# One tile for both accumulators of a spectral product, and scan rotations with a signed sine table (gated S5 + H3 mix, one core)

## The chip, the core and the metric

One core of one Trainium2 chip. The kernel is launched once; its time is the device time of that launch in microseconds (us), taken as the median of several runs. The kernel before takes 382.55 us (three runs, 381.49 to 382.69). A profile of one further execution gives each instruction's start and duration on the engines: PE (TensorE matmul), PEld (its weight loads), DVE (VectorE), ACT (ScalarE), POOL (GpSimd, which here mostly issues adding DMAs) and SP (the queue from which nearly all loads and stores are issued).

## What is computed

Two sequence mixers over 2048 steps and 1024 channels are blended by a gate. With `x` of shape [2048, 1024]:

```python
g   = sigmoid((x * gate_w).sum(-1))
# a: diagonal complex state space (S5), 1024 states
Bu  = x @ B_bar.T ;  h[t] = Lam_bar * h[t-1] + Bu[t] ;  a = 2 Re(h @ C.T) + x * Dskip
# b: H3: short convolution of k, times v, then a long convolution by FFT, times x
kv  = (4-tap conv of B_k) * B_v ;  b = x * (fftconv(kv, B_ssm_k) + kv * B_ssm_D)
out = g * a + (1 - g) * b
```

## The kernel before

**Order of work.** A helper `put` (line 92) chains every compute and queue instruction to the previous one of the same engine, so each engine runs its instructions in the order in which the Python code issues them; nothing is reordered later. Because all of them go through this helper, the profile names line 94 for nearly every row, and one tells groups apart by tile names. `move` and `load_t` (a DMA that transposes) go to SP's queue, `gather` is a DMA from POOL that adds its source into its destination.

**First half: H3, channel block by channel block (c = 0 to 7).** Per block of 128 channels the short convolution (`taps`), the spectra of kernel and signal (`fwd_K` into tile `Kh`, `fwd_V` into `Vh`), their complex block product, and the inverse transform (`inverse`, tile `psz`) are made. Both spectra have a real and an imaginary part (index `c`), four overlap blocks (`b`) and 512 columns. `products` (line 680) forms the product on DVE: accumulator `G` for the real part of K times V, accumulator `T2` (in the room of `BT[3]`) for the imaginary part. Each takes multiplies of 4096, 3072, 2048 and 1024 elements per partition and adds; one add, `G += n1`, is done by a `gather` DMA. Then `T2` is combined with `G`, and sum and difference of its halves are written to `G`, which `inverse` reads. It is a Python generator: each `yield` is a point at which the main loop (line 1136) puts other work of that block in between, `times_v` among it. `times_v` multiplies the convolved k by v (tile `ks`), mirrors it on PE (`lo`), makes `ev` on DVE and `ks += lo` by a `gather`; `fwd_V` on PE needs both. Kernel spectra of even blocks lie in `BT[2]`, of odd ones in the pool `kvh`. Interleaved with this are the first `Bu` products of the state space mixer and `turn_table` (line 461), in which ACT makes cosine and sine tables.

**Second half: S5.** Time is cut into four blocks (tb) of 512 steps, states into four groups (g) of 256. `Bu(i)` takes 32 matmuls of 512 columns per `i` (tile `both`, from `xT[tb]` and `BT[g]`); the list `order` (line 788) maps `i` to (tb, g). `turn_U` then adds the odd steps' neighbours to the even ones with ACT (`Q`) and two `gather`s (`U<-Q`). `scan` (line 913) rotates U by the cosine and sine tables, runs four recurrences (`tensor_tensor_scan`), rotates back into `hb` and updates the odd steps. `Cy` (tile `psy`) multiplies states by C. The lists `plan` and `turned` (lines 1390 to 1393) say which `Bu`, `turn_U` and `Cy` stand between scan j and scan j + 1.

**SP's queue around the change.** `xT` of time blocks 0 and 3 share one buffer (`xt_first`, line 78), so `load_xT(3)` waits for the last `Bu` with tb = 0. Before, `Bu(7)` is (0, 3), and `load_xT(3)` stands at line 1334, after `Bu(7)` and ahead of the last `inverse`, the loads of C (CT4 to CT7, lines 1353 to 1358) and the row loads `loads(0)` to `loads(2)`. `load_BT(3, ...)` stands at lines 1300 and 1301, ahead of the loads of C for states 1 to 3. `Bu(12)` is (3, 0), the first user of `xT[3]`; `plan` puts it at j = 3.

Of the kernel before, what the change touches and what calls it, by code (L numbers as in the profile page):

```python
# [20 lines left out]
def kernel(  # L21
# [115 lines left out]
    kv_pool = h3pool(h3, "kvh", 3)  # L137
    g_pool = h3pool(h3, "gh", 2)
    cv_pool = h3pool(h3, "cv", 2)
    tab_pool = h3pool(h3, "tab", 1)  # L140
    WK = h3pool(h3, "wkh", 1).tile([128, 2, 3072], BF16, name="wkh")
# [5 lines left out]
    zeros = WK[:, 0, 0:512]  # L147
# [254 lines left out]
    TCS = rot_pool.tile([128, NP, 2, HB], BF16, name="TCS")  # L402
    TC, TS = TCS[:, :, 0], TCS[:, :, 1]
# [72 lines left out]
    KH, VH, GH = {}, {}, {}  # L476
# [136 lines left out]
    def spectrum(which, c):  # L613
        if which == "K" and c % 2 == 0:

            t = BT[2].rearrange("p c d q -> p (c d q)")
        elif which == "G":
            t = whole[c] = g_pool.tile([128, 4096], BF16, name="G")
        else:
            t = kv_pool.tile([128, 4096], BF16, name=which + "h", tag="kvh")  # L620
# [59 lines left out]
    def products(c, h=0, home=u4, by_dma=True):  # L680

        if c not in GH:
            GH[c] = spectrum("G", c)
        K, Vt, G = (x[c][h].rearrange("p c b f d -> p c b (f d)") for x in (KH, VH, GH))
        w = K.shape[3]
        T2s = kv_pool.tile([128, 4096], BF16, name="t2", tag="kvh") if c == NC - 1 else BT[3].rearrange("p c d q -> p (c d q)")
        T2 = T2s[:, h * 2048:h * 2048 + 8 * w]
        W1, W2 = (WK[:, i, h * 1536:h * 1536 + 6 * w] for i in range(2))

        def mult(a, k, room, t=None):  # L690

            full = [128, 2, 4 - a, w]
            if t is None:
                t = room.rearrange("p (c b x) -> p c b x", c=2, x=w)
            tt(t, bc(K[:, k:k + 1, a:a + 1], full), Vt[:, :, 0:4 - a], ALU.mult)
            return t

        if c == 0 and h == 0:

            for f in range(2):  # L700
                k_, v_, g_ = (x[c][h][:, :, :, f] for x in (KH, VH, GH))
                tt(g_, bc(k_[:, 0:1, 0:1], [128, 2, 4, 128]), v_, ALU.mult)
        else:
            mult(0, 0, None, G)
        yield
        n1 = mult(1, 0, W1)
        if by_dma:
            gather(G[:, :, 1:], n1)
        yield
        t2 = mult(0, 1, T2)  # L710
        yield
        n2 = mult(1, 1, W2)
        if not by_dma:
            tt(G[:, :, 1:], G[:, :, 1:], n1, ALU.add)
        if c == NC - 1:
            yield
        n3 = mult(2, 1, home([128, 4 * w], BF16, "t"))
        tt(t2[:, :, 1:], t2[:, :, 1:], n2, ALU.add)
        n2 = mult(3, 1, home([128, 2 * w], BF16, "t"))
        tt(t2[:, :, 2:], t2[:, :, 2:], n3, ALU.add)  # L720
        n1 = mult(2, 0, W2[:, 0:4 * w])
        n3 = mult(3, 0, W2[:, 4 * w:])
        tt(t2[:, :, 3:], t2[:, :, 3:], n2, ALU.add)
        tt(n1[:, :, 1:], n1[:, :, 1:], n3, ALU.add)
        yield
        tt(G[:, :, 2:], G[:, :, 2:], n1, ALU.add)
        yield
        tt(t2[:, 1], G[:, 0], t2[:, 1], ALU.subtract)
        tt(t2[:, 0], G[:, 1], t2[:, 0], ALU.add)
        if c == 0 and h == 0:  # L730
            return
        lo, hi = ((t2[:, :, :, 0:256], t2[:, :, :, 256:512]) if c > 0 else
                  [T2s[:, i * 2048:(i + 1) * 2048].rearrange("p (c b x) -> p c b x", c=2, x=256) for i in range(2)])
        to = whole[c].rearrange("p (a c b x) -> p a c b x", a=2, c=2, b=4)
        tt(to[:, 0], lo, hi, ALU.subtract)
        tt(to[:, 1], lo, hi, ALU.add)

    def inverse(c):

        del GH[c]  # L740
        G = whole.pop(c).rearrange("p (a c b f d) -> p a c b f d", a=2, c=2, b=4, d=128)
        for par in range(2):
            ps = ps2([128, 2, 4, 128], "psz")
            for j in range(2):
                tl = 2 * par + j
                for fi in range(2):
                    for cc, tab in enumerate((CI, SI)):
                        mm(ps[:, j], tab[:, fi, tl * 128:(tl + 1) * 128], G[:, par, 1 - cc, :, fi],
                           fi == 0 and cc == 0, fi == 1 and cc == 1)
            cv = cv_pool.tile([128, 2, 4, 128], BF16, name="cv")  # L750
            act(cv, ps, func=ACT.Copy)
            move(cv_scr[c, :, 2 * par:2 * par + 2], cv)
            yield
# [34 lines left out]
    order = [(0, 0), (0, 1), (1, 0), (1, 1), (2, 0), (2, 1), (0, 2), (0, 3), (1, 2), (1, 3), (2, 2), (2, 3)]  # L788
# [16 lines left out]
    def Bu(i):  # L805
# [7 lines left out]
        if i in (10, 11):  # L813
            if i == 10:
                s5p["u2"] = xt_pool.tile([128, 2, 2 * (4 * HB + 4)], BF16, name="U2", tag="xT")
            U = s5p["u2"][:, i - 10]
# [96 lines left out]
    def scan(tb, g, fin):  # L913
# [4 lines left out]
        A = w2([128, 2, 2, HB], BF16, "A")  # L918
        W = None

        for js in ([slice(0, 1), slice(1, 2)] if last else [slice(0, 2)]):
# [6 lines left out]
            b = w2([128, 2, 2, HB], BF16, "trn")[:, :, js]  # L928
            tt(b, bc(TS[:, g2][:, None], full), Uj, ALU.mult)
# [4 lines left out]
            tt(Aj[:, 0], Aj[:, 0], b[:, 1], ALU.add)  # L934
            tt(Aj[:, 1], Aj[:, 1], b[:, 0], ALU.subtract)
            if W is None:
                W = w2([128, 2, 2, HB], BF16, "W")
            for j in range(js.start, js.stop):
                pi = 2 * g + j
                for c in range(2):  # L940
                    put("dve", V.tensor_tensor_scan, out=W[:, c, j], data0=bc(rv2[:, pi:pi + 1], [128, HB]),
                        data1=A[:, c, j], initial=0.0 if tb == 0 else init[tb][:, c, pi:pi + 1],
                        op0=ALU.mult, op1=ALU.add)
# [6 lines left out]
            Wj = W[:, :, js]  # L950
            tt(hb, bc(TC[:, g2][:, None], full), Wj, ALU.mult)
            if tb < NTB - 1:
                copy(WL[tb][:, :, g2], Wj[:, :, :, HB - 1])
            b = w2([128, 2, 2, HB], BF16, "trn")[:, :, js]
            tt(b, bc(TS[:, g2][:, None], full), Wj, ALU.mult)
            if not last:
                yield
            tt(hb[:, 0], hb[:, 0], b[:, 1], ALU.subtract)
            tt(hb[:, 1], hb[:, 1], b[:, 0], ALU.add)
# [4 lines left out]
            if by_act and tb == NTB - 1:  # L964
                q = [s5p["Q"].tile([128, 2, 2, HB], BF16, name="Q") for k in range(2)]
            else:
                q = [w2([128, 2, 2, HB], BF16, "q") for k in range(2)]
# [168 lines left out]
    for c in range(NC - 1):  # L1136
# [43 lines left out]
        steps(prod, 3)  # L1180
# [119 lines left out]
    load_BT(3, 0)  # L1300
    load_BT(3, 1)
# [4 lines left out]
    with tc.tile_pool(name="fin", bufs=1, side="right") as fin:  # L1306
# [16 lines left out]
        steps(prod, 2)  # L1323
        b6, b7 = Bu(6)
# [9 lines left out]
        load_xT(3)  # L1334
# [7 lines left out]
    wk = pool("wk", 5)  # L1342
# [5 lines left out]

    def w2(shape, dt, name):
        return wk.tile(shape, dt, name=name, tag="w2")  # L1350
# [39 lines left out]
    plan = ["", "B9 B10", "B11", "B12 B13 C0", "C1", "C2", "C3 B14", "B15", "G10", "G11", "G12 G13", "G20", "G21 G22 G23",  # L1390
            "", "", ""]
    turned = dict(zip(range(3, 12), (8, 9, 4, 10, 11, 12, 13, 14, 15)))
    turned[0] = 7
# [46 lines left out]
    for j in range(NS):  # L1440
# [109 lines left out]
```

## Time and profile before

| | value |
|---|---|
| median of 3 runs | 382.55 us |
| span of the profiled execution (first to last instruction) | 380.0 us |
| matmuls recorded on PE | 2435 |
| instructions on DVE | 595 |
| bytes moved by DMA | 71.78 MB |

A profile row of a group gives line, engine, operation, tiles (out<-in), shape (partitions x elements), count, then busy time in us, mean duration in ns, and the idle time before it with what ended it. A row of the timeline gives start, duration and count. Durations of neighbours on DVE overlap a little: an instruction starts some 80 ns before the one ahead of it is through, so steps are read from start to start. A matmul of 512 columns is listed with 379 ns, but the next one starts after 0.216 us.

### The profile page before, as it was taken

How to read it: one execution, taken by the hardware profiler on the slowest of the kernel's cores; microseconds unless marked ns; L12 is line 12 of the kernel's file. 1: busy time of each engine (PE TensorE's matmuls, PEld its weight loads, DVE VectorE, ACT ScalarE, POOL GpSimd, SP SyncE). 2: the span in 40 equal slices, each digit the busy share in tenths (PEclk: the TensorE clock that was granted, in tenths of full speed). 3: DMA queues.
4: the chain of work that ended last, by engine and by line, in shares of the span. 5: the costliest groups of instructions: out<-in, count | busy, mean ns of one | idle time of the engine just before them, and what ended most of it. 6: DMA issues, size and time to landing. Idle time of an engine off the chain costs nothing.

```text
span 380.0 us, 6673 instructions
## 1 busy us (share of the span) xinstructions
PE 371.0 (98%) x2435; PEld 201.2 (53%) x2469; DVE 369.6 (97%) x595; ACT 309.0 (81%) x475; POOL 78.9 (21%) x109
## 2 busy tenths in 40 slices
PE   8999999999999999999999999999999999999995
PEld 5656357575584856654454444444444444444444
DVE  8899999999999999999999999999999999999996
ACT  5879997988989999786949999996989769937621
POOL 4011030110301103021002012122415323635000
PEclk9999999999999999999999999999999999999999
DMA  7989999998999998969999999967899999999902
GB/s 168 167 112 248 213 216 227 219 195 206 226 175 192 227 177 170 184 145 151 194 206 190 204 209 253 240 137 135 158 226 181 237 254 220 153 255 155 218 0 110
DMA packets 126259, 71.78 MB, mean 189 GB/s; under 512 B 104649, under 2 KB 107601, under 8 KB 126226
## 3 DMA queue, kind: packets, MB, share of 16 engines
q1 hardware_dynamic: 112416, 45.90, 55.9%
q0 software_dynamic: 12688, 25.17, 38.9%
q10 hardware_dynamic: 1122, 0.28, 0.4%
q8 instruction: 19, 0.31, 0.3%
q14 instruction: 14, 0.11, 0.1%
HBM read 15.48 MB, written 8.39 MB: 63 GB/s over the span
## 4 chain that ended last, share of the span: by engine, by line
PE 44%; DMA 19%; DVE 17%; issue 11%; ACT 6%; POOL 1%; SPq 0%; DVEq 0%; POOLq 0%; ACTq 0%
PE both L94 16%; PE psk L94 7%; DMA U<-Q 5%; PE taps L94 5%; PE psv L94 5%; PE psz L94 4%; DMA kT<-in_B_k_dram 3%; DVE BT L94 3%; PE even L94 3%; DVE W L94 3%; PE odd L94 2%; PE foldk L94 2%; DMA ks<-lo 2%; DMA out_dram<-m 2%; DVE hb L94 2%
## 5 line engine op out<-in xcount | busy, mean ns | idle before, releaser
L94 PEld LDWEIGHTS <-BT 128*128 128x128 bf16 x640 | 62.1, 98 | 48.3 <-issue 0.2
L94 PE MATMUL both<-xT,BT 128*128 128x512 bf16 x375 | 83.0, 379 | 0.4
L94 POOL DMA_DIRECT2D U<-Q x26 | 26.4, 1027 | 82.5 <-ACT Q L94 39.9
L94 PEld LDWEIGHTS <-hb 128*128 128x128 bf16 x256 | 24.9, 98 | 30.2 <-issue 0.5
L94 PEld LDWEIGHTS <-U 128*128 128x128 bf16 x252 | 24.6, 98 | 27.4
L94 PE MATMUL psy<-CT,hb 128*128 128x512 bf16 x157 | 36.5, 379 | 0.1
L94 ACT ACTIVATE Vh<-psv 128x1024 bf16<-128x1024 f32 x32 | 30.7, 1034 | 6.2 <-PE psv L94 6.2
L94 PE MATMUL psy<-CT,U 128*128 128x512 bf16 (+1 forms) x156 | 34.7, 368 | 0.2
L94 ACT ACTIVATE U<-both 128x512 bf16<-128x512 f32 x44 | 24.2, 594 | 10.2 <-PE both L94 9.9
L94 DVE TENSOR_TENSOR_SCAN W<-rv,init,A 128x256 bf16<-128x256 f32 x48 | 32.2, 730 | 0.0
L94 POOL DMA_DIRECT2D G<-wkh x8 | 9.7, 1218 | 101.4 <-DVE wkh L94 101.4
L94 ACT ACTIVATE Q<-U,lam 128x512 bf16<-128x512 bf16 (+1 forms) x52 | 29.9, 612 | 0.0
L94 PE MATMUL psk<-eok,SF 128*128 128x384 bf16 (+1 forms) x119 | 28.2, 354 | 0.3
L94 PEld LDWEIGHTS <-SF 128*128 128x128 bf16 x184 | 18.0, 98 | 19.4 <-issue 0.7
L94 PE MATMUL psz<-G,CI 128*128 128x512 bf16 x64 | 24.3, 379 | 0.1
L94 PE MATMUL psz<-G,SI 128*128 128x512 bf16 x64 | 24.3, 379 | 0.0
L94 PE MATMUL taps<-dg,kT 128*128 128x128 bf16 (+1 forms) x352 | 22.2, 213 | 1.0 <-DMA kT<-kT 0.7
L94 PEld LDWEIGHTS <-kT 128*128 128x128 bf16 x352 | 21.7, 102 | 2.6 <-DMA kT<-in_B_k_dram 1.2
L94 PE MATMUL psy<-CTa,hb 128*128 128x512 bf16 x94 | 22.6, 379 | 0.2
L94 DVE TENSOR_TENSOR wkh<-BT,Vh 128x3072 bf16<-128x3072 bf16 (+4 forms) x20 | 21.8, 1109 | 0.0
L94 DVE TENSOR_TENSOR wkh<-Kh,Vh 128x3072 bf16<-128x3072 bf16 (+2 forms) x16 | 21.3, 1349 | 0.0
L94 PE MATMUL psy<-CTa,U 128*128 128x512 bf16 (+1 forms) x91 | 20.7, 370 | 0.1
(230 smaller groups left out, 838.0 us busy)
## 6 DMA issues: line engine op xcount, KB each, us to landing
U<-Q POOLq DMA_DIRECT2D x26, 256.0 KB, 4.9
G<-wkh POOLq DMA_DIRECT2D x6, 768.0 KB, 8.3
cv_scr<-cv SPq DMA_DIRECT2D x16, 256.0 KB, 6.0
kn<-in_B_ssm_k_dram SPq DMA_DIRECT2D x5, 512.0 KB, 4.5
v<-in_B_v_dram SPq DMA_DIRECT2D x5, 512.0 KB, 4.5
out_dram<-m SPq DMA_DIRECT2D x8, 256.0 KB, 4.3
BT<-cv_scr SPq DMA_DIRECT2D x7, 256.0 KB, 7.3
out_dram<-BT SPq DMA_DIRECT2D x7, 256.0 KB, 2.0
```

What stands on the lines that cost most here:

```text
L94: i = f(*a, **kw)
```

## The change

- `products`: both accumulators lie in one tile `sums` [128, 2, 4096]; each multiply covers real and imaginary part of K at once (8192, 6144, 4096 and 2048 elements). The `gather` still adds 3072 elements of the first accumulator; the second one's same add is done by DVE right behind it. Sum and difference go back into V's own tile, so the `G` pool is gone, and `kvh` has two buffers for V alone.
- Kernel spectra of odd blocks lie in `BT[3]`, so `load_BT(3)` moves behind the multiplies of the last block, after the loads of C 1 to 3.
- `turn_table` makes a second, negated sine table; `scan` uses both with the real and imaginary parts of its input swapped, so that each rotation is two multiplies and one full-width add (1024 elements) in place of two adds of 512. The recurrences write over their input, and the rotation tiles serve as room for the update of the odd steps.
- `order`: `Bu(6)`, `(7)`, `(8)` become (0, 2), (1, 2), (2, 2), and (0, 3), (1, 3), (2, 3) follow as `Bu(9)` to `(11)`. `plan` puts `Bu(9)` at j = 0, and `turned` puts its `turn_U` at j = 1. `load_xT(3)` moves to the end of j = 0.

```diff
-        T2s = kv_pool.tile(...) if c == NC - 1 else BT[3].rearrange("p c d q -> p (c d q)")
+        A = sums[:, :, h * 2048:h * 2048 + 8 * w].rearrange("p k (c b x) -> p k c b x", c=2, x=w)
+        def mult(a, t):
+            ...
+            k_ = bc(K[:, :, a:a + 1], [128, 2, 8 - 2 * a, w])
+            v_ = bc(Vt[:, :, 0:4 - a].rearrange("p c b x -> p c (b x)")[:, None], [128, 2, 2, (4 - a) * w])
+            tt(t, k_, v_, ALU.mult)
+            return t
...
+            mult(0, sums[:, :, h * 2048:h * 2048 + 8 * w])
+        yield
+        n1 = mult(1, WK[:, h * 3072:h * 3072 + 12 * w])
         if by_dma:
-            gather(G[:, :, 1:], n1)
+            gather(A[:, 0, :, 1:], n1[:, 0])
         yield
...
+        if by_dma:
+            tt(A[:, 1, :, 1:], A[:, 1, :, 1:], n1[:, 1], ALU.add)
+        else:
+            tt(A[:, :, :, 1:], A[:, :, :, 1:], n1, ALU.add)
+        yield
+        n2 = mult(2, WK[:, 3072:7168] if c > 0 else home([128, 8 * w], BF16, "t"))
+        n3 = mult(3, home([128, 4 * w], BF16, "t"))
+        yield
+        tt(n2[:, :, :, 1:], n2[:, :, :, 1:], n3, ALU.add)
+        tt(A[:, 1, :, 2:], A[:, 1, :, 2:], n2[:, 1], ALU.add)
+        yield
+        tt(A[:, 0, :, 2:], A[:, 0, :, 2:], n2[:, 0], ALU.add)
...
         act(y, h, func=ACT.Abs)
-        act(TS[:, 2 * g:2 * g + 2], h, func=ACT.Sin, scale=TWO_PI)
+        for k, sign in enumerate((1.0, -1.0)):
+            act(TSS[:, k, 2 * g:2 * g + 2], h, func=ACT.Sin, scale=sign * TWO_PI)
...
-            tt(Aj[:, 0], Aj[:, 0], b[:, 1], ALU.add)
-            tt(Aj[:, 1], Aj[:, 1], b[:, 0], ALU.subtract)
+            tt(Aj, Aj, bj, ALU.add)
...
-    order = [..., (0, 2), (0, 3), (1, 2), (1, 3), (2, 2), (2, 3)]
+    order = [..., (0, 2), (1, 2), (2, 2), (0, 3), (1, 3), (2, 3)]
...
-        steps(prod, 3)
+        steps(prod, 2)
         run(tv)
...
-    load_BT(3, 0)
-    load_BT(3, 1)
...
         steps(prod, 2)
+        load_BT(3, 0)
+        load_BT(3, 1)
         b6, b7 = Bu(6)
...
         run(turning[1])
-        load_xT(3)
         b10, b11 = Bu(8)
...
-    plan = ["", "B9 B10", "B11", "B12 B13 C0", ...]
+    plan = ["B9", "B10", "B11", "B12 B13 C0", ...]
...
+        if j == 0:
+            load_xT(3)
```

More of the change, by code (lines that the diff above doesn't have):

```diff
@@ L134, in h3pool @@
         return st.enter_context(tc.tile_pool(name=name, bufs=bufs, **kw))
-    kv_pool = h3pool(h3, "kvh", 3)
-    g_pool = h3pool(h3, "gh", 2)
+    kv_pool = h3pool(h3, "kvh", 2)
+    sums = h3pool(h3, "acc", 1).tile([128, 2, 4096], BF16, name="acc")
     cv_pool = h3pool(h3, "cv", 2)
     tab_pool = h3pool(h3, "tab", 1)
-    WK = h3pool(h3, "wkh", 1).tile([128, 2, 3072], BF16, name="wkh")
+    WK = h3pool(h3, "wkh", 1).tile([128, 7168], BF16, name="wkh")
     ld = pool("ld", 3, side="right")
@@ L401 @@
     lamd = {}
-    TCS = rot_pool.tile([128, NP, 2, HB], BF16, name="TCS")
-    TC, TS = TCS[:, :, 0], TCS[:, :, 1]
+    TCS = rot_pool.tile([128, 3, NP, HB], BF16, name="TCS")
+    TC, TSS = TCS[:, 0], TCS[:, 1:]
     cs = {}
@@ L613, in spectrum @@
     def spectrum(which, c):
[L614 to L618, printed above, removed]
+        if which == "K":
+            t = BT[2 + c % 2].rearrange("p c d q -> p (c d q)")
         else:
-            t = kv_pool.tile([128, 4096], BF16, name=which + "h", tag="kvh")
+            t = whole[c] = kv_pool.tile([128, 4096], BF16, name="Vh", tag="kvh")
         k = 2 if c == 0 else 1
@@ L680, in products @@
     def products(c, h=0, home=u4, by_dma=True):
-        if c not in GH:
-            GH[c] = spectrum("G", c)
-        K, Vt, G = (x[c][h].rearrange("p c b f d -> p c b (f d)") for x in (KH, VH, GH))
+        K, Vt = (x[c][h].rearrange("p c b f d -> p c b (f d)") for x in (KH, VH))
         w = K.shape[3]
[L686 to L695, printed above, removed]
+        A = sums[:, :, h * 2048:h * 2048 + 8 * w].rearrange("p k (c b x) -> p k c b x", c=2, x=w)
+        def mult(a, t):
+            if len(t.shape) == 2:
+                t = t.rearrange("p (k y) -> p k y", k=2)
+            t = t.rearrange("p k (c b x) -> p k c b x", c=2, x=w)
+            k_ = bc(K[:, :, a:a + 1], [128, 2, 8 - 2 * a, w])
+            v_ = bc(Vt[:, :, 0:4 - a].rearrange("p c b x -> p c (b x)")[:, None], [128, 2, 2, (4 - a) * w])
+            tt(t, k_, v_, ALU.mult)
             return t
@@ L700, in products @@
             for f in range(2):
-                k_, v_, g_ = (x[c][h][:, :, :, f] for x in (KH, VH, GH))
-                tt(g_, bc(k_[:, 0:1, 0:1], [128, 2, 4, 128]), v_, ALU.mult)
+                k_, v_ = (x[c][h][:, :, :, f] for x in (KH, VH))
+                full = [128, 2, 8, 128]
+                tt(A.rearrange("p k c b x -> p k (c b) x")[:, :, :, f * 128:(f + 1) * 128], bc(k_[:, :, 0:1], full),
+                   bc(v_.rearrange("p c b d -> p (c b) d")[:, None], full), ALU.mult)
         else:
-            mult(0, 0, None, G)
+            mult(0, sums[:, :, h * 2048:h * 2048 + 8 * w])
@@ L730, in products @@
+        tt(A[:, 1, 0], A[:, 0, 1], A[:, 1, 0], ALU.add)
         if c == 0 and h == 0:
             return
-        lo, hi = ((t2[:, :, :, 0:256], t2[:, :, :, 256:512]) if c > 0 else
-                  [T2s[:, i * 2048:(i + 1) * 2048].rearrange("p (c b x) -> p c b x", c=2, x=256) for i in range(2)])
+        t2 = sums[:, 1]
+        if c > 0:
+            lo, hi = (A[:, 1, :, :, i * 256:(i + 1) * 256] for i in range(2))
+        else:
+            lo, hi = (t2[:, i * 2048:(i + 1) * 2048].rearrange("p (c b x) -> p c b x", c=2, x=256) for i in range(2))
@@ L787 @@
     Us = {}
-    order = [(0, 0), (0, 1), (1, 0), (1, 1), (2, 0), (2, 1), (0, 2), (0, 3), (1, 2), (1, 3), (2, 2), (2, 3)]
+    order = [(0, 0), (0, 1), (1, 0), (1, 1), (2, 0), (2, 1), (0, 2), (1, 2), (2, 2), (0, 3), (1, 3), (2, 3)]
     order += [(NTB - 1, g) for g in range(NG)]
@@ L917, in scan, with turned @@
         Ve, Uo = Us[tb, g]
-        A = w2([128, 2, 2, HB], BF16, "A")
-        W = None
+        A = wk.tile([128, 2, 2, HB], BF16, name="A")
+        def turned(o, i, js):
+            tt(o, TSS[:, :, 2 * g + js.start:2 * g + js.stop], i[:, ::-1], ALU.mult)
+        b = None
         for js in ([slice(0, 1), slice(1, 2)] if last else [slice(0, 2)]):
@@ L927, in scan @@
                 yield
-            b = w2([128, 2, 2, HB], BF16, "trn")[:, :, js]
-            tt(b, bc(TS[:, g2][:, None], full), Uj, ALU.mult)
+                b = wk.tile([128, 2, 2, HB], BF16, name="trn", bufs=1)
+            bj = b[:, :, js]
+            turned(bj, Uj, js)
             if js.start == 0:
@@ L940, in scan @@
                 for c in range(2):
-                    put("dve", V.tensor_tensor_scan, out=W[:, c, j], data0=bc(rv2[:, pi:pi + 1], [128, HB]),
+                    put("dve", V.tensor_tensor_scan, out=A[:, c, j], data0=bc(rv2[:, pi:pi + 1], [128, HB]),
                         data1=A[:, c, j], initial=0.0 if tb == 0 else init[tb][:, c, pi:pi + 1],
@@ L949, in scan @@
             hb = hbs[tb, g][:, :, js]
-            Wj = W[:, :, js]
-            tt(hb, bc(TC[:, g2][:, None], full), Wj, ALU.mult)
+            tt(hb, bc(TC[:, g2][:, None], full), Aj, ALU.mult)
             if tb < NTB - 1:
-                copy(WL[tb][:, :, g2], Wj[:, :, :, HB - 1])
-            b = w2([128, 2, 2, HB], BF16, "trn")[:, :, js]
-            tt(b, bc(TS[:, g2][:, None], full), Wj, ALU.mult)
+                copy(WL[tb][:, :, g2], Aj[:, :, :, HB - 1])
+            turned(bj, Aj, js)
             if not last:
                 yield
-            tt(hb[:, 0], hb[:, 0], b[:, 1], ALU.subtract)
-            tt(hb[:, 1], hb[:, 1], b[:, 0], ALU.add)
+            tt(hb, hb, bj, ALU.subtract)
             by_act = tb * NG + g in scaled_by_act or last and js.start == 0
@@ L963, in scan @@
                 product(0)
-            if by_act and tb == NTB - 1:
+            if by_act:
                 q = [s5p["Q"].tile([128, 2, 2, HB], BF16, name="Q") for k in range(2)]
             else:
-                q = [w2([128, 2, 2, HB], BF16, "q") for k in range(2)]
+                q = A, b
             def scaled(q=q):
```

41 lines of the change are left out of this document (9 added, 32 removed).

## The prediction, made before the changed kernel ran

> **What bounds the kernel now.** I read the busy times and the forty slices first, then the stages, then what PE waited for.
>
> ```profile
> span 380.0 us, 6673 instructions
> PE 371.0 (98%) x2435; PEld 201.2 (53%) x2469; DVE 369.6 (97%) x595; ACT 309.0 (81%) x475; POOL 78.9 (21%) x109
> ```
> ```profile
> 220.00:230.00 10.00, 9.95 (x47) 4.51 (x46) 9.86 (x24) 9.94 (x15) 0.86 (x1) 1.00 1.21 193
> 230.00:240.00 10.00, 9.95 (x47) 4.57 (x47) 9.79 (x19) 9.90 (x15) 3.71 (x5) 1.00 1.15 247
> 370.00:380.00 10.00, 6.01 (x43) 4.12 (x42) 6.46 (x10) 1.80 (x2) 0.00 (x0) 0.96 0.28 105
> ```
> ```profile
> PE taps L94 <- DMA kT<-kT: 0.7, 1, 0.7
> PE psv L94 <- DMA ks<-lo: 0.7, 1, 0.7
> PE mirror L94 <- DVE ks L94: 0.4, 1, 0.4
> ```
> ```profile
> L94 PE MATMUL both<-xT,BT 128*128 128x512 bf16 x375 | 83.0, 379 | 0.4
> ```
>
> PE and DVE are both nearly full, but only one of them is the floor. PE is busy 371.0 of 380.0 us; in 220 to 240 it begins 47 matmuls per 10 us, one each 0.213 us, with no pause. (The table's columns are length, PE, PEld, DVE, ACT, POOL, granted clock, DMA share, GB/s.) PE's work does not change, since the matmuls are the same ones, some in another order. Its idle 9.0 us lie mostly in the last ten us (10.00 less 6.01). After the first microseconds PE waited 0.7 + 0.7 + 0.4 us, and 0.7 of that is a transfer of kT that the change does not touch. So a faster DVE can give **at most about 1.1 us**, and a new wait on PE is lost in full: nothing later could take it up.
>
> **The change, part by part.**
>
> *DVE's products.* Five instructions of seventeen go per block; the elements stay.
>
> ```profile
> 69.87 2.28 DVE L94 TENSOR_TENSOR G<-BT,Vh 128x4096 bf16<-128x4096 bf16 x1
> 72.08 1.75 DVE L94 TENSOR_TENSOR wkh<-BT,Vh 128x3072 bf16<-128x3072 bf16 x1
> 73.74 2.28 DVE L94 TENSOR_TENSOR BT<-BT,Vh 128x4096 bf16<-128x4096 bf16 x1
> 75.95 0.68 DVE L94 TENSOR_TENSOR ev<-ks,lo 128x1024 bf16<-128x1024 bf16 x1
> 76.55 1.75 DVE L94 TENSOR_TENSOR wkh<-BT,Vh 128x3072 bf16<-128x3072 bf16 x1
> 78.22 1.21 DVE L94 TENSOR_TENSOR t<-BT,Vh 128x2048 bf16<-128x2048 bf16 x1
> 79.35 1.75 DVE L94 TENSOR_TENSOR BT<-BT,wkh 128x3072 bf16<-128x3072 bf16 x1
> ...
> 85.81 1.23 DVE L94 TENSOR_TENSOR G<-G,wkh 128x2048 bf16<-128x2048 bf16 x1
> ```
>
> From start to start 4096 elements take 2.21 us and 2048 take 1.13, so 0.53 ns an element and some 0.06 us an instruction. Nine half or whole blocks with five instructions fewer save 9 x 5 x 0.06 = 2.7 us of DVE; by whole durations, which overlap, each costs 0.15 and the saving is 6.8.
>
> *DVE's scans.* Two adds of 512 become one of 1024, twice in 16 scans.
>
> ```profile
> L94 DVE TENSOR_TENSOR A<-TCS,U 128x1024 bf16<-128x1024 bf16 x14 | 9.6, 684 | 0.0
> ```
> ```profile
> L94 DVE TENSOR_TENSOR A<-A,trn 128x512 bf16<-128x512 bf16 x30 | 11.3, 419 | 0.2
> ```
>
> 2 x 419 less 684 is 154 ns in durations, 32 times 4.9 us; by steps (11.3/30 x 2 = 0.75 against 0.60, less the new wait of the recurrence on the add just ahead) 0 to 0.15 us each. I take 2 us. DVE's relief is thus 5 us, bounds 2 and 12, all of it under PE: worth 0 to 1.1 us, and I take 0.4, the mirror wait.
> The Trainium skill (VectorE: DVE Perf Modes, "The TRN2 errata") puts a fixed cost of about 150 cycles, 0.156 us, on each instruction, paid once by a large tile and again by every small one. That is what the whole durations show and the starts do not; by the rule DVE gains the full 12 us (an estimate), the shortfall in the next part would be covered, and the sum would be 397.5 in place of 400.0.
>
> *The product's adding DMA loses cover.*
>
> ```profile
> G<-wkh POOLq DMA_DIRECT2D x6, 768.0 KB, 8.3
> ```
> ```profile
> G<-wkh POOLq DMA_DIRECT2D x1, 768.0 KB, 8.9
> ...
> ks<-lo POOLq DMA_DIRECT2D x1, 256.0 KB, 8.4
> ```
>
> The median is the page's, the other two are from 143 to 160 us. Before, `wkh` is ready at 72.08 + 1.75 = 73.83 and `G` is needed at 85.81: 12.0 us of cover for 8.3. After, between the two stand `ev` 0.60, an add of 3072 (1.67), multiplies of 4096 and 2048 (2.21 + 1.13), two adds of 2048 (2.26): 7.9 us. The shortfall is 0.4 to 1.0 us a block, about what the block saves; DVE comes out level there.
> Also `ev` moves back: it began 6.1 us into the block (75.95 less 69.87), and after comes behind 8192 and 6144 elements, 4.3 + 3.3 = 7.6 us. So `ks += lo` starts 1.5 us later and directly behind the 768 KB transfer. PE already waited 0.7 us for that landing once. I take 2.5 us more on PE, bounds 0 and 6.
>
> *ACT's second sine table.*
>
> ```profile
> L94 ACT ACTIVATE TCS<-hr 128x512 bf16<-128x512 f32 x4 | 2.6, 642 | 0.0
> ```
>
> Four more of 642 ns in blocks where ACT has few gaps and evicts PSUM for PE: 0 to 2.6 us, I take 0.5.
>
> *The load of xT for time block 3.* This is the large one. SP's queue before, and PE's chain beside it:
>
> ```profile
> 205.82 6.70 SPq L94 DMA_TRANSPOSE xT<-in_A_x_dram  x2
> 215.50 2.05 SPq L94 DMA_DIRECT2D cv_scr<-cv  x2
> 217.78 1.30 SPq L94 DMA_TRANSPOSE CT<-in_A_C_re_dram  x1
> ...
> 224.49 0.47 SPq L94 DMA_DIRECT2D pbb<-cv_scr  x1
> ...
> 226.57 3.28 SPq L94 DMA_TRANSPOSE CT<-in_A_C_re_dram  x1
> ...
> 238.74 1.17 SPq L94 DMA_DIRECT2D xr<-in_A_x_dram  x1
> 241.21 0.38 SPq L94 DMA_DIRECT2D BT<-cv_scr  x1
> ```
> ```profile
> 212.69 3.45 PE psz L94 x16
> 216.41 10.74 PE both L94 x49
> ```
> ```profile
> BT<-in_A_B_re_dram SPq DMA_TRANSPOSE x1, 5.7
> ```
> ```profile
> xr<-in_A_x_dram SPq DMA_DIRECT2D x3, 256.0 KB, 8.7
> ...
> CT<-in_A_C_im_dram SPq DMA_TRANSPOSE x4, 7.1
> ```
>
> Before, the two transposes go out at 205.82. PE ends the last `psz` at 212.69 + 3.45 = 216.1 and runs Bu(9), (10), (11), each 32 matmuls of 83.0/384 = 0.216 us (375 of 384 are recorded), 6.9 us; Bu(12) = (3, 0) begins at **216.1 + 20.8 = 236.9**. (The load at 241.21, which waits for the 20th matmul of Bu(12), agrees: 236.9 + 4.3.)
> After, the slots on PE stand in the same order, with (0, 3), (1, 3), (2, 3) in Bu(9) to (11). But (0, 3) reads the shared buffer until 216.1 + 6.9 = 223.0, and in SP's program the load now stands behind the last stores of `cv`, eight transposes of C and seven row loads. The head of that queue is tied to PE, since `cv` comes out of `psz`. SP was through with them at 238.74 + 1.17 = 239.9, without a pause. So: first half at 239.9, second 6.70/2 = 3.35 later at 243.3, landed 7.1 later (the CT transposes of this stretch) at **250.4**. PE would wait 250.4 less 236.9 = **13.5 us**. Both halves are needed, as each matmul reads all 512 columns.
> Bounds: with every C transpose at 1.30 and every row load near 0.5, SP is there at 217.78 + 14 = 231.8, and with 3.35 and 5.7 us it lands at 240.8: 3.9 us. With the 8.7 us that the row loads took, 252: 15.1. The DMA share of 1.21 and 1.15 in that stretch speaks for the upper half; that xT's own transposes and two adds of Q are gone from its beginning speaks for a microsecond or two less.
> ```profile
> 187.92 2.28 DVE L94 TENSOR_TENSOR G<-Kh,Vh 128x4096 bf16<-128x4096 bf16 x1
> ```
>
> BT(3) itself is needed only at 216.1. Its room is free when the last products, begun here, have read K: 8192, 6144, 6144, 4096 and 2048 elements, 4.3 + 3.3 + 3.3 + 2.2 + 1.1 = 14.2 us, at 202.1; two transposes and 5.7 us to land end near 212. That is covered, by 4 us, and if the cover went, its lateness would move Bu(9) and all behind it.
>
> *PE's clock after the wait.*
>
> ```profile
> L94 PE MATMUL raised<-wkh 128*128 128x512 bf16 x6 | 2.9, 626 | 1.2 <-DVE magic L94 1.2
> ```
>
> No wait of over 2 us stands in the trace after the start, so this is bounded: nothing, or what the first six matmuls from rest cost, 6 x (626 less 379) = 1.5 us. I take 1.5, the one row of PE after rest.
> The Trainium skill (TensorE: Matmul & The Clock Gate, "What's actually happening") says that an idle window of about 3.4 us drops the array to 1.2 GHz until about 3.4 us of work have passed; by it the loss is half of that, 1.7 us (an estimate), and the sum 400.2. The row shows the slow start, and no row here shows a fall after a wait.
>
> **Sum.** Against the profiled execution: 380.0 - 0.4 + 2.5 + 0.5 + 13.5 + 1.5 = 397.6 us of span. The median lies 2.55 us above the span: 400.15, so **400.0 us**.
>
> **The rivals.**
> - *The queue runs freely.* With the 1 MB of xT gone from 205 to 215, the loads of C flow and the wait is 2 to 7 us. For it: six transposes of C went out in a row without much wait, the first and the last of them
>
> ```profile
> 191.84 1.30 SPq L94 DMA_TRANSPOSE CTa<-in_A_C_re_dram  x1
> ...
> 200.39 1.29 SPq L94 DMA_TRANSPOSE CT<-in_A_C_im_dram  x1
> ```
>
> in 9.8 us. Against: row loads and POOL's adds share the same engines, share 1.15 to 1.21. 380.0 + 4.5 + 1 + 2.55 = **388**.
> - *Faster.* xT(3) lands before 236.9, for which SP must reach it by 236.9 - 5.7 - 3.35 = 227.9, 12 us sooner than before; and DVE's lead removes the 0.7 and 0.4 us waits. Then **381.4**. Against: even the queue's fastest rows give 231.8.
> - *DVE's new operands are slow.* If the reads with swapped parts and two repeated dimensions ran at half rate, each `trn` multiply of 1024 would cost what 2048 does, 0.53 us more, 32 times 17 us; DVE, 97% full, would become the bound of the second half. Of that some 8 us outlast the wait for xT: **408**. Nothing speaks for it but that no row shows such reads; repeated operands already run at full rate in the multiplies above.
> - *The change gives DVE no time*, since starts overlap: 400 stays, as PE sets the end.
>
> **How the numbers follow.** Forecast 0.72; free queue 0.13; slow operands 0.06; faster 0.05; a wait so short that only the small terms stay, within 0.3%, 0.04. A difference of 0.3%, 1.15 us, is about what a measurement of this kernel tells from none. So faster 0.05, same 0.04, slower 0.91. The range: the low end takes the 3.9 us wait with no other cost, 382.55 + 3.9 = 386.5; the high end 15.1 with 6 in the blocks, 2.6 on ACT and 1.5 of clock, 407.8, cut to 407.
>
> **What would show it.** Right: a single wait of PE (or PEld) on DMA xT<-in_A_x of 8 to 15 us near 240; SP's xT transposes behind `xr` loads; matmuls over 0.3 us apart right after; DVE idle in the second half. A `ks<-lo` wait near 155 of over 2 us shows the block term. Wrong: no such wait, or SP at xT before 232, takes away the main term; DVE busy over 370 us or `trn` rows over 1 us would show the slow operands.

## The result and the profile after

The changed kernel takes **404.6 us** (median of four runs, 402.25 to 417.97) against 382.5 us beside it: 1.0567 times the time before, with a 95% interval of 1.0519 to 1.0616. It is slower by some 22 us; 400.0 was forecast, between 386.5 and 407.

The execution that was profiled with the result is the 417.97 us one, a slow run that the ratio leaves out, so the rows of after come from a second profile of the same kernel (405.98 us, span 404.2), which is set beside the 380.0 us span of before. First its busy times and the forty slices of PE and of PE's clock:

```profile
span 404.2 us, 6632 instructions
...
PE 375.5 (93%) x2469; PEld 200.3 (50%) x2469; DVE 369.5 (91%) x515; ACT 312.7 (77%) x479; POOL 80.8 (20%) x109
...
PE   7999899999999997999899990399999999999996
...
PEclk9999999999999999999999997599999999999999
```

PE has a hole of two slices (10.1 us each) behind 242 us, and its clock falls in the hole and comes back only after it. DVE has 80 instructions fewer than before (515 for 595) and is busy for the same 369.5 us (369.6). What PE waited for, in us in total, times and longest:

```profile
PE both L94 <- DMA xT<-in_A_x_dram: 16.1, 1, 16.1
PE psv L94 <- DMA ks<-lo: 2.8, 1, 2.8
PE both L94 <- DMA BT<-in_A_B_im_dram: 1.2, 1, 1.2
...
PE psz L94 <- DVE Vh L94: 1.2, 1, 1.2
...
PE psk L94 <- ACT cv L94: 0.9, 3, 0.4
PE mirror L94 <- DVE ks L94: 0.8, 3, 0.4
```

One wait, for the last load of x, is larger than all others together. SP's queue shows how it came about:

```profile
221.39 2.05 SPq L94 DMA_DIRECT2D cv_scr<-cv  x2
...
240.70 0.61 SPq L94 DMA_DIRECT2D xr<-in_A_x_dram  x1
241.41 13.49 SPq L94 DMA_TRANSPOSE xT<-in_A_x_dram  x2
```

The two transposes stand behind the last stores of cv, the loads of C and the row loads, as the prediction had it, and go out at 241.4. Before they took 6.70 us to issue, now 13.49: the first goes out at 241.4, the second at 245.7, and the latter lands 13.0 us later, at 258.7. PE resumes at 258.81.

The rest of the rows of after that count are on DVE. A block's products, from one block in the middle:

```profile
71.18 4.42 DVE L94 TENSOR_TENSOR acc<-BT,Vh 128x8192 bf16<-128x8192 bf16 x1
75.51 3.35 DVE L94 TENSOR_TENSOR wkh<-BT,Vh 128x6144 bf16<-128x6144 bf16 x1
...
83.38 1.22 DVE L94 TENSOR_TENSOR t<-BT,Vh 128x2048 bf16<-128x2048 bf16 x1
84.63 1.23 DVE L94 TENSOR_TENSOR wkh<-wkh,t 128x2048 bf16<-128x2048 bf16 x1
85.89 2.36 DVE L94 TENSOR_TENSOR acc<-acc,wkh 128x2048 bf16<-128x2048 bf16 x2
...
90.68 2.36 DVE L94 TENSOR_TENSOR Vh<-acc 128x2048 bf16<-128x2048 bf16 x2
```

From 71.18 to 90.68 + 2.36 = 93.04 this is 21.9 us. Before, the same work went from 69.87 (in the prediction's rows) to the end of this row,

```profile
89.47 2.36 DVE L94 TENSOR_TENSOR G<-BT 128x2048 bf16<-128x2048 bf16 x2
```

91.83: 22.0 us. Five instructions went, and with them 0.1 us. The starts tell why: the multiply `t` and the add that reads it start 1.25 us apart, the add and its reader 1.26, while before the multiply `t` (78.22 in the prediction's rows), whose result the next instruction did not read, was followed after 1.13 us. From 60 to 200 us, in both profiles, every instruction of 2048 elements with no pause behind it is followed after 1.13 to 1.14 us by one that, by the code, does not need it, and after 1.25 to 1.26 by one that does. So an instruction that needs the one directly ahead of it (reads its result, or writes over what it reads) pays some 0.12 us. By the code the new chain of 12 has five such steps, the old one of 17 had three: the 5 x 0.06 us that the prediction priced are all but eaten by 2 x 0.12. The scans say the same. One whole scan, from one `A<-TCS,U` to the next, before and after:

```profile
216.73 0.68 DVE L94 TENSOR_TENSOR A<-TCS,U 128x1024 bf16<-128x1024 bf16 x1
...
225.72 0.69 DVE L94 TENSOR_TENSOR A<-TCS,U 128x1024 bf16<-128x1024 bf16 x1
```
```profile
227.87 0.68 DVE L94 TENSOR_TENSOR A<-TCS,U 128x1024 bf16<-128x1024 bf16 x1
...
236.98 0.69 DVE L94 TENSOR_TENSOR A<-TCS,U 128x1024 bf16<-128x1024 bf16 x1
```

8.99 us before, 9.11 after. (The two adds of 512 did not need each other, and the first half of the recurrence could start when the first of them was through.)

### The profile page after: what moved, and what is told of

It is laid out like the page before. It is cut to its first block, busy times and chain, and to the rows that moved or that the text cites. A ratio compares the mean times of both kernels' runs of the same rounds, so it can differ in the third digit from the quotient of the medians.

```text
span 416.2 us, 6632 instructions
## 1 busy us (share of the span) xinstructions
PE 377.2 (91%) x2469; PEld 201.6 (48%) x2469; DVE 369.4 (89%) x515; ACT 312.7 (75%) x479; POOL 79.9 (19%) x109
## 4 chain that ended last, share of the span: by engine, by line
PE 58%; issue 15%; DMA 13%; DVE 12%; SPq 1%; ACT 0%; POOL 0%; POOLq 0%
PE psy L94 27%; PE both L94 21%; DMA xT<-in_A_x_dram 6%; DVE acc L94 5%; DMA acc<-wkh 5%; DVE wkh L94 3%; PE psz L94 2%; PE psv L94 2%; DMA ks<-lo 2%; PE psk L94 2%; SPq L94 1%; PE taps L94 1%; PE foldk L94 1%; DVE t L94 1%; DVE Vh L94 1%
## 5 line engine op out<-in xcount | busy, mean ns | idle before, releaser
L94 PE MATMUL both<-xT,BT 128*128 128x512 bf16 x384 | 86.0, 386 | 29.0 <-DMA xT<-in_A_x_dram 29.0
L94 ACT ACTIVATE U<-both 128x512 bf16<-128x512 f32 x44 | 24.2, 594 | 31.7 <-PE both L94 31.4
L94 DVE TENSOR_TENSOR wkh<-BT,Vh 128x6144 bf16<-128x6144 bf16 (+2 forms) x16 | 43.0, 2688 | 0.2
L94 DVE TENSOR_TENSOR acc<-BT,Vh 128x8192 bf16<-128x8192 bf16 (+2 forms) x10 | 35.6, 3568 | 0.5 <-ACT Vh L94 0.3
L94 POOL DMA_DIRECT2D acc<-wkh x8 | 9.7, 1218 | 124.0 <-DVE wkh L94 124.0
L94 DVE TENSOR_TENSOR_SCAN A<-rv,init,A 128x256 bf16<-128x256 f32 x48 | 32.2, 733 | 0.5
L94 DVE TENSOR_TENSOR acc<-acc,wkh 128x2048 bf16<-128x2048 bf16 (+3 forms) x23 | 32.3, 1430 | 0.3
L94 ACT ACTIVATE BT<-psk 128x1024 bf16<-128x1024 f32 x31 | 30.0, 1035 | 2.6 <-PE psk L94 2.6
L94 PEld LDWEIGHTS <-SF 128*128 128x128 bf16 x184 | 18.2, 99 | 21.9 <-issue 3.7
L94 PE MATMUL psz<-Vh,CI 128*128 128x512 bf16 x64 | 24.3, 379 | 1.2 <-DVE Vh L94 1.2
L94 PE MATMUL psz<-Vh,SI 128*128 128x512 bf16 x64 | 24.3, 379 | 0.0
L94 DVE TENSOR_TENSOR A<-TCS,U 128x1024 bf16<-128x1024 bf16 (+1 forms) x16 | 10.4, 653 | 15.4 <-PE psz L94 8.4
```

Of the source, the lines that this page charges most:

```text
L94: i = f(*a, **kw)
```

## The experiments

The theory to test was **A**: SP reaches the last load of x late, PE waits for it, and this is most of the loss. Its rivals: **B**, the blocks' products, slow operands or the tables make it; and, once the wait was taken away, several sources for what remained. Ratios are against the kernel before on the same chip. In all, the kernel before took 381.6 to 382.2 us beside them.

**The changed kernel again** (no edit).

> The changed kernel once more, unedited, for a second profile. If the wait of PE for the last load of x (xT, time block 3) is a fixed part of the change, it is there again, single, near 242 us of the span, and 13 to 30 us long; all other waits of PE stay under 3 us each. If it belongs to that one execution, it is under 8 us here and the time is still near 403.

405.98 us; PE's wait is 16.1 us, up to 258.8, and no other exceeds 2.8. It belongs to the change. This is the profile shown above.

**The kernel before with the load late.**

```diff
-        load_xT(3)
         b10, b11 = Bu(8)
...
+        if j == 0:
+            load_xT(3)
```

> The kernel before with one line moved: the load of xT for time block 3 is issued at the end of scan 0, behind the loads of C and the row loads, instead of after Bu(7). The order of the Bu products, the products on DVE, the scans and the tables stay as before. Theory A (the place in SP's queue makes most of the loss): PE waits 13 to 25 us for that load, and the time is 396 to 406. Theory B (the loss comes from the blocks, the new operands on DVE or the tables): the wait is hidden or small, and the time is 383 to 387.

402.15 us, 1.0533 times before (1.0489 to 1.0578).

```profile
span 397.8 us, 6705 instructions
```
```profile
PE both L94 <- DMA xT<-in_A_x_dram: 16.6, 1, 16.6
```

One line moved in the old kernel gives a wait of the same length and a loss of some 20 us, with none of the new instructions in it. A holds as far as it goes. What is left for all else in the change is 2.5 us by the two medians, 1.3 by the two ratios and 6.4 by the two spans; the intervals of the ratios overlap, and single runs of either kernel lie up to 4 us apart.

**The changed kernel with the load early.** Bu(9) is written ahead of the second half's loads, and the load stands directly behind it.

```diff
     load_CT(5)
+    for b in Bu(9):
+        run(b)
+    load_xT(3)
     loads(0)
...
-        if j == 0:
-            load_xT(3)
-    plan = ["B9", "B10", ...]
+    plan = ["", "B10", ...]
```

> The changed kernel with Bu(9) written ahead of the second half's loads and the load of xT for time block 3 right behind it, ahead of the row loads and of the loads of C for states 6 and 7 (it then stands behind the loads of C for states 4 and 5). Theory A: the load goes out near 230 and lands by 240 to 245 or a little after Bu(12) is due; the wait of PE is 0 to 6 us, the slow matmuls after it go too, and the time is 384 to 391. Theory B: the time stays at 396 or above.

395.7 us, 1.0370 (1.0318 to 1.0422): both expectations missed. The wait for xT is gone, yet 14 us stay.

```profile
PE psy L94 <- ACT U L94: 4.0, 1, 4.0
PE psv L94 <- DMA ks<-lo: 2.6, 1, 2.6
PE both L94 <- ACT U L94: 1.9, 1, 1.9
PE psz L94 <- DVE Vh L94: 1.3, 1, 1.3
```

Two kinds are left: waits in the blocks (2.6 and 1.3), and two new ones near 250 and 260 on ACT's evictions of Bu (1.9 and 4.0), which are not there beside the long wait. The next runs take them in turn.

**The same with ev early in every block.**

```diff
-        steps(prod, 2)
+        step(prod)
         run(tv)
+        step(prod)
```

> As the run with the early load, and besides in every block ev and the adding DMA ks += lo go ahead of the product's second multiply, as they went behind the two first ones before. If the later ks += lo in the blocks costs PE the 2.5 us that the prediction took, this is 1.5 to 4 us faster than the run with the early load alone; if PE was not held up by it, the two are within 1 us.

395.8 us, 1.0327 (1.0252 to 1.0401): no difference that shows, as the intervals overlap. Its profile is of the 398.12 us execution, the longest of the four. There the wait for `ks<-lo` is gone, but PE waits 3.8 us for `Vh` (1.3 before the edit). That fits a DVE so full that an instruction put forward sets another back; no run shows that this is the reason.

**The scans in a room of their own.** In the change the scans' tiles lie over V's pool, and the last inverse transform reads V, since the product is now written back there. Scan 0 waits for it (DVE, after):

```profile
211.14 2.36 DVE L94 TENSOR_TENSOR Vh<-acc 128x2048 bf16<-128x2048 bf16 x2
222.06 0.69 DVE L94 TENSOR_TENSOR A<-TCS,U 128x1024 bf16<-128x1024 bf16 x1 [8.57 <-PE psz L94]
```

Before, scan 0 began at 210.98 without a pause. The edit puts them over the tile of the sums:

```diff
-                hbs[tb, g] = s5p["hb"].tile([128, 2, 2, HB], BF16, name="hb")
+                hbs[tb, g] = hb_pools[len(hbs) % 7].tile([128, 2, 2, HB], BF16, name="hb")
...
+    s5p["io"] = pool("io", 2)
     wk = pool("wk", 2)
-    s5p["hb"] = pool("hb", 7)
+    hb_pools = [pool("hb", 5)] * 5 + [pool("hb2", 2)] * 2
     s5p["Q"] = pool("Q", 4)
     s5p["uu"] = pool("uu2", 2)
-    s5p["io"] = pool("io", 2)
```

> The run with the early load, and the scans' rooms laid over the tile of the sums instead of over V's pool. There the first scan stood 7.4 us still for the last inverse transform, which reads V, and PE then waited 4.2 and 2.1 us near 250 to 260 (395.7 us). Theory A2 (those two waits and the slow matmuls behind them are the late scans): scan 0 starts near 214, right behind the last product, the two waits go, and the time is 386 to 390. Theory B2 (they come from something else, such as the loads of C or ACT's own queue): the time stays at 394 or above.

397.05 us, 1.0327 (1.0271 to 1.0382): A2 falls, and the two waits are still there (1.9 and 5.4 us). Scan 0 does start at once, but scan 3 then stands still (DVE, this run):

```profile
212.98 0.69 DVE L94 TENSOR_TENSOR A<-TCS,U 128x1024 bf16<-128x1024 bf16 x1
...
251.21 0.69 DVE L94 TENSOR_TENSOR A<-TCS,U 128x1024 bf16<-128x1024 bf16 x1 [9.96 <-DMA U<-Q]
```

It waits for the states of (0, 3), now Bu(9), whose turn_U ran long before it was needed in the old order.

**Products alone**: the last run with the old scans, one sine table and a separate output of the recurrence (the scans' rooms still lie over the tile of the sums, but are divided otherwise).

```diff
-        for k, sign in enumerate((1.0, -1.0)):
-            act(TSS[:, k, 2 * g:2 * g + 2], h, func=ACT.Sin, scale=sign * TWO_PI)
+        act(TS[:, 2 * g:2 * g + 2], h, func=ACT.Sin, scale=TWO_PI)
...
-            tt(Aj, Aj, bj, ALU.add)
+            tt(Aj[:, 0], Aj[:, 0], b[:, 1], ALU.add)
+            tt(Aj[:, 1], Aj[:, 1], b[:, 0], ALU.subtract)
...
-                    put("dve", V.tensor_tensor_scan, out=A[:, c, j], ...
+                    put("dve", V.tensor_tensor_scan, out=W[:, c, j], ...
```

> The run with the scans' own room, but with scans and tables as before: one sine table, adds of 512 elements, a separate output of the recurrence. What is left of the change is the products and the order. If the signed table and the full-width adds relieve DVE by the 2 us of the prediction or more and this matters, it is slower by up to 2 us; if the second table on ACT costs PE 0.5 to 2.6 us in the blocks, it is faster by that; if a full-width add that must wait for the instruction ahead costs as much as two half adds, the two are within 0.5 us.

397.13 us, 1.0391 (1.0346 to 1.0435): the medians agree within 0.1 us, the ratios lie 2.4 us apart with intervals that overlap. So signed table, full-width adds and in-place scans cost nothing that shows; a gain of up to some 2 us is not excluded.

**Own room, ev early in block 5 alone**, the block in which PE waits for `ks<-lo`.

```diff
+        step(prod)
+        if c == 5:
+            run(tv)
+        step(prod)
-        steps(prod, 2)
         run(tv)
```

> The run with the scans' own room, and in channel block 5 alone ev and the adding DMA ks += lo go ahead of the product's second multiply. If the 2.7 us wait of PE for ks near 157 is lost in full, this is 1 to 3 us faster; if DVE, level with PE in the blocks, only moves the wait on to the next psz, the two are within 1 us.

394.19 us, 1.0293 (1.0254 to 1.0331); 2.9 us by the medians, but the intervals of the ratios overlap. In the profiles the wait at 156 is gone and that for `psy` is 2.8 us (5.4 in the run without this edit).

**The changed kernel with the scans' own room only**: the edit of the pools above, and the load of x late.

> The changed kernel with only the scans' rooms moved from V's pool to the tile of the sums; the load of xT stays late. If the still first scan is hidden under PE's wait for xT, the time stays within 2 us of the changed kernel (403 to 406), although DVE's 8.6 us of idle time near 222 go; if it is exposed, it is 396 to 399.

407.59 us, 1.0633 (1.0583 to 1.0683): above the 403 to 406 that were expected, but its interval overlaps that of the changed kernel (1.0519 to 1.0616). It is not faster. The 8.6 us of DVE near 222 are gone and 9.8 us before scan 3 (`DMA U<-Q`) stand in their place; PE waits 14.7 us for xT.

**turn_U of (0, 3) right behind scan 0**, on top of the run with ev early in block 5.

```diff
-    turned = dict(zip((1, *range(3, 12)), (9, 7, ...
+    turned = dict(zip((0, *range(3, 12)), (9, 7, ...
```

> The run with the scans' own room and the early ev in block 5, and turn_U for (0, 3) right behind scan 0 instead of in two parts around j = 1. There its second adding DMA landed at about 250 and scan 3 stood 6 to 10 us still for it, and PE's first product with C behind that. Theory A3 (the new order of the Bu products makes the states of (0, 3) late, and this is what is left beside the blocks): scan 3 no longer waits over 2 us, PE's waits near 247 and 256 shrink to under 1.5 us in all, and the time is 386 to 390. Theory B3 (DVE or ACT are simply too full there): the waits stay in sum above 4 us, and the time is 392 or more.

392.75 us, 1.0312 (1.0266 to 1.0357): A3 falls as stated. Scan 3 no longer waits, but PE still waits 1.9 and 4.5 us on ACT's evictions, so these waits do not come from the late states of (0, 3).

**The order alone**: the kernel before with the order of the Bu products, `plan`, `turned` and the place of one buffer (U2) as in the changed kernel with the early load, and the load early.

```diff
-    order = [..., (0, 2), (0, 3), (1, 2), (1, 3), (2, 2), (2, 3)]
+    order = [..., (0, 2), (1, 2), (2, 2), (0, 3), (1, 3), (2, 3)]
```

> The kernel before, with its own products, scans and tables, and only the order of the Bu products changed as in the change: (0, 3) as Bu(9), its turn_U around j = 1; the load of xT stands early, as in the run with the early load. Theory A3: the order alone costs the late states of (0, 3), a wait of scan 3 of 5 to 10 us and of PE of 4 to 8 us with slow matmuls behind: 388 to 392, and the products and scans are not needed for it. If instead the waits come with the new products or scans, it stays within 382 to 385.

388.63 us, 1.0181 (1.0156 to 1.0206), as expected of the order; scan 3 stands still for 6.1 us.

```profile
PE psy L94 <- ACT U L94: 4.5, 1, 4.5
PE both L94 <- ACT U L94: 1.9, 1, 1.9
```

With the old products and scans both waits are there. The order makes them, and 6.9 us in all (0.0181 of 382.2; 6 to 8 by the interval). The difference to the changed kernel with the early load, 1.0370 less 1.0181 or 7.2 us (5 to 9 by the intervals), is what products, scans and rooms cost in that pair of runs.

**turn_U early, the scans over V's pool as in the change**: the run with turn_U early, with the edit of the pools taken back.

```diff
-    s5p["io"] = pool("io", 2)
     wk = pool("wk", 2)
-    hb_pools = [pool("hb", 5)] * 5 + [pool("hb2", 2)] * 2
+    s5p["hb"] = pool("hb", 7)
     ...
+    s5p["io"] = pool("io", 2)
```

> As the run with the early turn_U, but with the scans' rooms over V's pool, as the change has them: scan 0 waits 7 us for the last inverse transform again. If DVE has that much time to spare before PE needs the states of scan 3, the time is within 1 us of the run with the early turn_U; if not, PE waits 3 to 6 us near 255 and the time is 3 to 8 us longer.

390.97 us, 1.0225 (1.0198 to 1.0252). DVE stands still for 5.1 us before scan 0 and PE does not pay for it; the run with the room of its own is even the slower one, which neither expectation had. Part of it is on record: in that run ACT waited 1.6 us for a row load (`pbb<-cv_scr`) that this one had in time, and PE's wait for `psy` was 4.5 us, here 2.8. Why the load came late there is open.

**The order alone, without the load of x.**

```diff
-    load_xT(3)
+    xTs[3] = xTs[0]
```

> The run with the order alone, with the load of xT for time block 3 left out altogether: the products of that block read block 0's x instead, so that 1 MB less is moved and nothing waits for it. Theory C (what remains of the loss with the early load, 6.4 us, is the crowd of transfers between 220 and 255): the loads and adds behind it land sooner, PE's waits near 242 and 251 (2.1 and 4.7 us) fall below 3 us in sum, and the time is 383 to 385.5. Theory D (what remains is ACT's order of work: it stands 4.6 us still between 216 and 222, because the outputs of Bu(9) come later than those of (0, 3) did, and is full from there on): the two waits stay above 4.5 us in sum, and the time is 387 to 389.

387.56 us, 1.0162 (1.0125 to 1.0199).

```profile
PE psy L94 <- ACT U L94: 2.8, 1, 2.8
PE both L94 <- ACT U L94: 1.9, 1, 1.9
```

One megabyte less is worth some 1 us by the medians and 0.7 by the ratios, whose intervals overlap. The waits sum to 4.7 instead of 6.4, so by its own measure D holds and C does not. C has a share, though: in the run with the order alone ACT waited 1.6 us for a row load just ahead of its four scalings, and without the load of x it does not; the wait for `psy` shrank by 1.7 us. That the remaining 4.7 come from ACT's order of work is read from ACT's rows; no run changed that order by itself. The rows before and in the run with the order alone:

```profile
240.54 2.19 ACT L94 ACTIVATE m<-CT,mc2i 128x1024 bf16<-128x1024 bf16 x2
242.61 0.60 ACT L94 ACTIVATE U<-both 128x512 bf16<-128x512 f32 x1
...
243.83 2.18 ACT L94 ACTIVATE m<-CT,mc2i 128x1024 bf16<-128x1024 bf16 x2
```
```profile
218.66 0.22 ACT L94 ACTIVATE U<-lam 128x4 bf16<-128x4 f32 x1 [2.25 <-DVE q L94]
...
222.36 0.60 ACT L94 ACTIVATE U<-both 128x512 bf16<-128x512 f32 x1 [2.36 <-PE both L94]
...
247.61 1.15 ACT L94 ACTIVATE pbb<-pbb,omg 128x1024 bf16<-128x1024 bf16 x1 [1.56 <-DMA pbb<-cv_scr]
...
249.71 4.25 ACT L94 ACTIVATE m<-CT,mc2i 128x1024 bf16<-128x1024 bf16 x4
...
255.33 2.06 ACT L94 ACTIVATE U<-both 128x512 bf16<-128x512 f32 x4
```

Before, ACT turned (0, 3) from 217 to 220 and later put the scaling of C (`m`) between evictions of Bu. In the new order it stands idle 2.25 us (for DVE) and 2.36 us (for PE's Bu(9)) at that time, since the outputs of (0, 3) do not exist yet, and four scalings in a row stand ahead of the eviction for which PE waits. How much is the lost 4.6 us and how much the lost places between the products was not told apart.

Not tried: a buffer of its own for the last load of x, which would have left everything else of the change, and the new products in the old order, which need another 8 KB a partition for K (4096 values of two bytes). No version of the change beat the kernel before; the fastest that holds it whole is the last but one, with load, turn_U and one ev early, 390.97 us.

## Why the prediction was right, and where it was not

*The load of xT (+13.5, with 8 to 15 as its sign): right in kind, too small at 16.1 measured, and this near partly by luck.* The moved line alone makes a loss of that kind. Its start was met within 1.5 us (241.41; 239.9 was worked out), but by two misses that cancel: the stores of cv went out 5.9 us later (221.39 for 215.50), and SP took 20.0 us for the queue behind them, not 24.4. The kernel before with only the load late has neither miss, and there the working holds better: SP reached the load at 238.75, the second half went out 6.4 us later (3.35 had been taken) and landed after 7.5 (7.1 had been taken). In the changed kernel the landing is off: 13.0 us behind the second issue were measured, and the issue itself took 13.49 us, not 6.70. The windows between (length, PE, clock, DMA share, GB/s) show the transfers crawl:

```profile
244.00:245.00 1.00, 0.00 (x0) 1.00 1.01 275
245.00:246.00 1.00, 0.00 (x0) 1.00 1.38 55
246.00:247.00 1.00, 0.00 (x0) 1.00 1.45 139
247.00:248.00 1.00, 0.00 (x0) 0.55 1.10 73
```

From 245 on the DMA engines are busier than the microsecond before and move a fifth to a half of what they moved in it. Four adding DMAs of POOL (CT, CT, U, pbb) went out between 241.6 and 246.3 and took 10.5 to 11.5 us each. That PE also came 5.7 us later than in the sum (242.6, not 236.9) kept the wait at 16.1 us instead of 22: two more errors that offset each other.

*The blocks (+2.5 and +0.5): right for `ks<-lo` and ACT, short by what had not been seen.* The last inverse transform starts 5.9 us later on PE than before (before, after, and the wait for BT):

```profile
212.53 0.38 PE L94 MATMUL psz<-G,CI 128*128 128x512 bf16 x1
```
```profile
199.41 19.17 PE L94 MATMUL both<-xT,BT 128*128 128x512 bf16 x88 [1.22 <-DMA BT<-in_A_B_im_dram]
218.41 0.38 PE L94 MATMUL psz<-Vh,CI 128*128 128x512 bf16 x1
```

The waits make it up: `ks<-lo` 2.8 (2.1 more), `Vh` 1.2, BT 1.2, `psk` for ACT's evictions into `cv` 0.9, the mirror 0.4 more: 5.8. The waits for `Vh` and for BT had not been seen. The latter is BT(2), the operand of Bu(6), whose load the change did not move; it is not there in the run with the early load. BT(3), which the prediction called covered by 4 us, was in time. That the 0.9 us come from the second sine table fits the run of the products alone, which has one table and no such wait. The bound of 6 for the adds and 2.6 for ACT holds. The shortfall of 0.4 to 1.0 us a block behind the product's adding DMA did not come: the adds landed after 6.6 us in the median, not 8.3, and DVE waited for one of them once, 0.3 us.

*The mirror (-0.4) and DVE's relief of 5 us, bounds 2 to 12: wrong.* The step that failed is the price of an instruction from starts of neighbours that did not depend on each other; more steps of the new chains depend. The relief is 0.1 us a block in the products and -0.12 us in a scan, and DVE's busy time stays (369.6 and 369.5): below the lower bound. Since DVE's time was costed at nothing on the way to the end, the sum lost only 0.4 by it. The rival "no time for DVE" was the true one, and it stands beside the forecast, not against it. The fixed cost per instruction that the Trainium skill states (VectorE: DVE Perf Modes, "The TRN2 errata") would have given 12 us by the prediction's estimate. The rows here do not bear that out: 17 instructions take 22.0 us and 12 take 21.9.

*The clock (+1.5): right in kind, 2.6 measured.* Rows of after behind the wait:

```profile
263.00:264.00 1.00, 1.00 (x4) 0.50 0.04 4
264.00:265.00 1.00, 1.00 (x6) 0.92 0.00 0
265.00:266.00 1.00, 1.00 (x7) 1.00 0.00 0
```

From 258.81 on the starts are 0.36 to 0.43 us apart for 13 matmuls, until 264.2, and then 0.216: 5.4 us for what takes 2.8 at full speed.

*Sum.* 5.9 + 16.1 + 2.6 = 24.6, against 404.2 - 380.0 = 24.2 of span in this profile. (The prediction put PE's 9.0 us of idle time before mostly into the last ten us; it is 4.0 of the 9.0. Nothing in the sum hangs on it.) The rival of slow operands is out: `trn` multiplies take 0.69 us as before, and DVE's busy time is unchanged. That of the free queue was half true: SP's queue went in 20.0 us instead of 24.4, but not because the 1 MB of x was gone from 205 to 215. With only that load moved it took 24.0 (214.79 to 238.75), and in the change the late stores and the landing took the gain back.

What the prediction did not have at all is what stood behind the wait. It treated the order of the Bu products as neutral for PE ("the slots on PE stand in the same order"); with the load early the order still costs 6.9 us through ACT, and scan 0 and scan 3 stand still for 5 to 10 us on DVE. In the change itself the long wait covers this: with the scans' own room and the load late, scan 0 starts at once and no time is gained.

## What to carry to other kernels

When a change reuses a buffer, follow the buffer: here K in the room of BT(3) forced a new order of products, and that put a 1 MB load behind a full queue; the arithmetic that was meant to be saved had no part in the largest term. Price an instruction by the steps of a chain that depends as yours will, not by neighbours that overlap. And when one wait is taken away, count on a second behind it: taking the 16 us wait away gained 9 (404.6 to 395.7).

## What the runs showed of the hardware

- **Transposing loads beside adding DMAs.** The same two transposes of x, 1 MB, landed 17.3 us after the first issue (61 GB/s) with four 256 KB adds in flight, and the adds took 10.5 to 11.5 us, against 4.8 to 5.1 for the same four in the run without the load. The size varies: with the scans' own room the pair took 15.2 us beside the same four adds, and these 6.0 to 7.8; in the kernel before with the load late it took 13.9. Which kind holds back the other no run here separates. The Trainium skill (Advanced Engine Details and Errata, "X-Bar Transpose (TRN2)") has transposes as fast as other transfers, at 350 to 400 GB/s; between 240 and 260 us of the changed kernel all transfers together stay below 300 GB/s in every half microsecond.
- **PE's clock can fall some 4 us after a wait began, when the wait is over by then.** In the run without the load PE stops at 252.4 and resumes at 255.3:

```profile
255.00:256.00 1.00, 0.72 (x4) 1.00 0.35 61
256.00:257.00 1.00, 1.00 (x5) 0.68 1.09 190
257.00:258.00 1.00, 1.00 (x3) 0.50 0.15 27
```

The first five steps from start to start are 0.216 us, then eight are 0.41 to 0.43: a wait of 2.8 us costs 1.7 more. The run with the scans' own room and ev early in block 5 shows the same after its 2.8 us wait for `psy`. The 2.8 us wait for `ks<-lo` at 156 in the changed kernel is followed by no slow start. The Trainium skill (TensorE: Matmul & The Clock Gate, "What's actually happening") has an idle window of about 3.4 us that runs on by itself, whatever the kernel does. That would make it chance where in a window a wait falls, but not that a wait of 2.8 us, shorter than the window, is enough, as it was here twice. How long the half clock lasts did not follow the length of the wait: 5.4 us of work after 16.1 us, 5.8 after the 4.0 us of the run with the early load, 2.9 after the 4.5 us of the order alone.
